# Two attention layers on one core: how exponent products, scores and projection copies are dealt out near the end and the beginning of the attention phase

## The chip, the cores and the metric

The kernel runs on one core of a Trainium2 chip. The metric is the device time of one execution in microseconds; lower is better. The engines are named as the profile names them: PE (TensorE matmuls; PEld are its weight loads), DVE (VectorE), ACT (ScalarE), POOL (GpSimd) and SP (SyncE, which issues most DMAs).

## The reference, cut to what matters

`x` has 2048 tokens of 576 features. Four residual steps follow each other: attention, a spectral filter, attention, a spectral filter. Everything that the change touches lies in the attention step:

```
h   = layernorm(x)
q,k,v = (h @ wqkv) split in 32 heads of 18
s   = q k^T * 18**-0.5, kept where 0 <= query - key < 256
x   = x + (softmax(s) v) @ wo
```

The spectral step is `x + irfft2(rfft2(layernorm(x)) * W)`.

## The kernel before, in words

`layer_a` is one attention layer and is run twice. Tokens are cut into 16 tiles of 128, heads into 8 groups of four (`NQ`). A work item is numbered x = 16 n + j: group n, tile j; there are NX = 128 of them. A head is addressed by `pair` and `hp`; `hp` chooses rows 0 to 63 or 64 to 127 of the PE array, so that two neighbouring matmuls of different `hp` run side by side.

Each score is computed twice. `score_max(x, pair, hp)` (tile `S`, line 1172) multiplies 128 queries by up to 384 keys, and DVE takes the masked row maximum (line 1174). When the four tiles of a chunk have their maxima, `m_rows(n, c)` turns them with one PE transpose (`tpm`, line 1185), ACT negates them into `mt` (line 1187), and two DMAs (line 1189, from SP) write them as an extra row of the stacked queries `qs`. `exps(x, pair, hp)` (tile `E`, line 1205) multiplies 128 keys by the queries of tiles x, x+1 and x+2; that extra row subtracts the maximum, and ACT takes the exponent (line 1206) into a tile `P`. So exponents of x need the maxima of tile x+2, by way of that transpose, ACT and DMA. In the order listings `E118_0` is the product for x = 118; its second number is 2·hp + pair, and `S124_1_0` is x, pair, hp. `tpm7_2` is the transpose of group 7, chunk 2, that is of tiles 120 to 123.

`part` multiplies `P` with the values into the bank `U` (line 1225); after each fourth tile DVE transposes `U` into `us` (line 1230). `divide`, `back` and `store` scale it, turn it back (`o`) and send it off; for group 7 `store` is four DMAs from SP into `o7` (line 1254). `pack` copies group results inside DRAM (line 1258), and `attended` loads them (`oraw`).

The projections of q and k for later groups are cut into units of 14 matmuls into a bank `pj` (line 1109). After a unit, ACT copies it (line 1121, and for later units a second copy, line 1124), and a remainder is subtracted by DVE or POOL (line 1127) and stored.

PSUM has eight banks: three for `S`, three for `E` (some projection units and transposes use them too), one `pj`, one `U`.

All engines run in the order in which the program records work. `opening` records the scores of the first LEAD = 10 items and 70 projection matmuls. `bursts` then records bursts: one score, three exponent products, two scores (scores run ten items ahead), after which come value products, pieces of projection units and, from burst 139 on, when the projections are all done, value products alone. There are 158 bursts; they cover exponents up to x = 117 (MIX = 118) and all scores. The tail loop (from line 1440 on) records the exponents of x = 118 to 127, four at a time, with the value products two tiles behind. Then `out.early` begins the output projection (`ops`, line 802). `behind(t)` is called as the exponents of t are recorded, and issues the loads and splits for the output projection (lines 744 to 780).

Of the kernel before, what the change touches and what calls it, by code (L numbers as in the profile page):

```python
# [8 lines left out]
F32 = mybir.dt.float32  # L9
F32R = mybir.dt.float32r  # L10
BF = mybir.dt.bfloat16
AF = mybir.ActivationFunctionType
# [3 lines left out]
S, D = 2048, 576  # L16
# [699 lines left out]
class Out:  # L716
# [149 lines left out]
def layer_a(tc, ident, eps, bp, big, src, dst, wqk_d, wv_d, wo_d, dc_d, gc_d, dram, copy, wvs, second, spectral, share):  # L866

    nc = tc.nc
    V, A, T, P = nc.vector, nc.scalar, nc.tensor, nc.gpsimd
# [14 lines left out]
    if True:  # L884
# [191 lines left out]
        with ExitStack() as c2:  # L1076
            wp = c2.enter_context(tc.tile_pool(name="a2", bufs=2))
            pp = Banks(tc, c2, "a2p", ("S", "pj"))
# [10 lines left out]
            ended = []  # L1089

            def remainders():
                while ended:
                    ended.pop(0)()

            def proj(i, c, bank=0):

                box = {}
                ks = k_steps()
                cs = slice(c * 512, c * 512 + 512)

                def mm(s, k):
                    wk, p, xk = k
                    if s == 7 and c == 2 and 0 < i < 8:
                        w_split(i + 1)
                    if s == 0:
# [3 lines left out]
                    T.matmul(box["ps"].rearrange("r (n p) -> r n p", n=NT) if second else box["ps"], w[:, wk], x, start=s == 0, stop=s == len(ks) - 1)  # L1109
                    if s == len(ks) - 1:  # L1110
                        if 4 * i + c < 12:

                            sg = wp.tile([128, 4, 384], F32, tag="P", name=f"sg{i}_{c}", bufs=6)
                            sg = sg.rearrange("r a b -> r (a b)")[:, 0:1024].rearrange("r (a t) -> r a t", a=2).bitcast(F32R)
                        else:
                            sg = wp.tile([128, 2, 512], F32R, tag="sg", name=f"sg{i}_{c}", bufs=2)
                        by, rest = box["ps"], sg
                        if second:
                            by = by.rearrange("r (n p) -> r p n", n=NT)
                            rest = sg.rearrange("r a (p n) -> r a p n", n=NT)  # L1120
                        A.copy(rest[:, 0], by)  # L1121
                        aside = 4 * i + c >= 14
                        if aside:
                            A.copy(rest[:, 1].bitcast(F32), by)

                        def remainder():
                            (P if aside else V).tensor_sub(sg[:, 1] if aside else rest[:, 1], sg[:, 1].bitcast(F32) if aside else by,  # L1127
                                                           (sg if aside else rest)[:, 0].bitcast(F32))

                            (nc.scalar if i < 2 else nc.sync).dma_start(qk_d[:, 128 * i:128 * i + 128, cs].rearrange("a r t -> r a t").bitcast(F32), sg.bitcast(F32))  # L1130
                        ended.append(remainder)
                return [lambda s=s, k=k: mm(s, k) for s, k in enumerate(ks)]

            vts = {}
# [55 lines left out]

            pt = {}

            def exps(x, pair, hp):
# [9 lines left out]
                ps = pp.tile([128, 512], F32, name=f"E{x}_{hl_}", **(dict(tag="S", bufs=3) if pair and NX - LEAD <= x else dict(tag="E", bufs=3)))  # L1203
                b = 64 * hp
                T.matmul(ps[:, 0:nq], k[b:b + 64, pair, j * 128:j * 128 + 128], q[b:b + 64, pair, j * 128:j * 128 + nq], start=True, stop=True)  # L1205
                A.activation(p[:, hl_, 0:nq], ps[:, 0:nq], AF.Exp, scale=SC)  # L1206
# [7 lines left out]
            us = {}  # L1214

            def part(x, half):
                n, i = divmod(x, NT)
# [107 lines left out]
            def source(p):  # L1325
                x, half = p
                i = x % NT
                return x - 1 if half == 0 else x - 2 + 2 * (i % 2)

            def bursts():  # L1330

                es = [(x, pair, hp) for x in range(MIX) for pair in range(2) for hp in range(2)]
                ss = [(x + LEAD, pair, 1 - hp) for x, pair, hp in es]
                parts = [(x, half) for x in range(MIX - 2) for half in range(2) if x % NT]
                values = {(4 * x + 7) // 3 + 2 for x in range(0, MIX - 2, 2)}
                ends = [3] + [max(k - 1 for k in values if k - 1 <= 4 + 134 * (i + 1) // 22) for i in range(22)]
                unit = {k: i for i, end in enumerate(ends) for k in range(ends[i - 1] + 1 if i else 0, end + 1)}
                at = 70
                for k in range(-(-len(es) // 3)):
                    e, c = es[3 * k:3 * k + 3], ss[3 * k:3 * k + 3]  # L1340
# [9 lines left out]
                    remainders()  # L1350

                    new, took = [], 0
                    spread = at == len(pj)
                    while parts and (took < 430 or source(parts[0]) < e[0][0] - 3 if spread else took == 0 or parts[0][0] % 2 or parts[0][1]):
                        if (4 * source(parts[0] if spread else (parts[0][0] | 1, 1)) + 3) // 3 + 2 > k:
# [10 lines left out]
                    tasks = [] if took and not spread or 3 * k + 3 >= len(es) else due[:1]  # L1366
                    del due[:len(tasks)]
                    n = 0
                    if k in unit and k not in values:
# [10 lines left out]
                        yield f  # L1380
                    at += n

                    full = (3 * k + len(e)) // 4 + LEAD - 1
# [18 lines left out]
            def behind(t):  # L1402
# [14 lines left out]
                if t - OB + 8 in range(0, 10, 2):  # L1417
                    out.load_x(((t - OB + 8) // 2 + 1) % 5)
# [16 lines left out]
            V.memset(U, 0.0)  # L1435
            for f in bursts():
                f()
                done += 1
            now = -(-4 * MIX // 3)
# [86 lines left out]
```

## Time and profile before

| what | value |
|---|---|
| median of 3 runs | 1331.53 us (1329.79 to 1331.54) |
| the profiled execution's own time | 1330.75 us |
| its span, first to last instruction | 1328.8 us |
| first layer: bursts from, value products end | 127.9, 456.6 us |
| second layer: bursts from, value products end | 806.4, 1136.4 us |
| PE busy | 1294.7 us (97%) |

A busy PE is not a PE at its peak, since the ends of matmuls are modelled: a wait shorter than the length of a matmul does not show as idle time. It shows as a later start, so starts are compared rather than gaps.

### The profile page before, as it was taken

Reading aid. Unit: us, or ns where it says so; the run is one execution under the profiler, and the core shown is the slowest. Engines: PE = TensorE matmul, PEld = TensorE weight load, DVE = VectorE, ACT = ScalarE, POOL = GpSimd, SP = SyncE. Lnnn points to the kernel's source line nnn. Section 1 sums busy time; section 2 is a strip of 40 time slices with the busy share of each in tenths; the row PEclk is TensorE's granted clock in tenths of the full one; section 3 lists DMA queues with packets and bytes.
Section 4 is the critical chain, followed back from the end, with each engine's and each line's share of the span. In section 5 each row is a group of like instructions: output and inputs, shape, how many; then the busy total and the mean of one; then the engine's idle time right before and its main releaser. Section 6 shows DMA issues by size and latency. Waiting matters only on the chain.

```text
span 1328.8 us, 33094 instructions
## 1 busy us (share of the span) xinstructions
PE 1294.7 (97%) x10911; PEld 956.4 (72%) x10911; DVE 948.4 (71%) x3136; ACT 753.1 (57%) x1896; POOL 714.1 (54%) x1200
## 2 busy tenths in 40 slices
PE   9999999999999999999999999999999999899998
PEld 8986666666665599975999975666666654798587
DVE  5417888888889587766674158888888887575855
ACT  5622776777767645543355325677766778574233
POOL 3258566776667443467221295567667667213821
PEclk9999999999999899999999999999999999999999
DMA  6857665765557737688873468566556658497874
GB/s 205 215 156 204 221 199 188 235 195 185 189 163 240 220 116 228 197 274 254 282 246 76 103 207 220 189 213 185 181 176 195 188 173 280 141 336 267 297 253 163
DMA packets 179487, 274.22 MB, mean 206 GB/s; under 512 B 67743, under 2 KB 77727, under 8 KB 177989
## 3 DMA queue, kind: packets, MB, share of 16 engines
q1 hardware_dynamic: 167007, 243.63, 58.5%
q0 software_dynamic: 4656, 13.44, 4.0%
q10 hardware_dynamic: 7654, 15.03, 3.3%
q8 instruction: 88, 1.44, 0.5%
q14 instruction: 82, 0.67, 0.2%
HBM read 164.54 MB, written 114.81 MB: 210 GB/s over the span
## 4 chain that ended last, share of the span: by engine, by line
PE 86%; DVE 5%; issue 3%; DMA 3%; ACT 2%; SPq 1%; POOL 0%; DVEq 0%; ACTq 0%; POOLq 0%
PE pj L1109 20%; PE S L1172 13%; PE U L1225 12%; PE vps L1005 9%; PE ops L802 6%; PE E L1205 6%; PE po L274 4%; PE pq L524 3%; PE p L503 2%; PE pf L274 2%; PE pi L600 2%; PE pz L312 1%; DVE jk L1174 1%; PE tpm L1185 1%; DVE us L1230 1%
## 5 line engine op out<-in xcount | busy, mean ns | idle before, releaser
L1174 DVE CUSTOM_DVE_ANT_0 jk<-S,mask 128x384 bf16<-128x384 f32 (+2 forms) x1024 | 488.5, 526 | 72.4 <-PE S L1172 38.0
L1206 ACT ACTIVATE P<-E 128x384 f32<-128x384 f32 (+2 forms) x1024 | 407.7, 479 | 171.0 <-PE E L1205 130.1
L1172 PE MATMUL S<-ks,qs 63*128 63x384 f32 (+2 forms) x1024 | 280.7, 374 | 3.5 <-DVE m L1174 1.3
L1208 POOL TENSOR_SCALAR_AFFINE_SELECT P<-P 128x512 f32<-128x512 f32 x256 | 163.3, 638 | 195.4 <-ACT P L1206 183.6
L1172 PEld LDWEIGHTS S<-ks,qs 63*128 63x128 f32 x1024 | 146.2, 184 | 117.8 <-DVE m L1174 89.3
L1205 PE MATMUL E<-qs,ks 64*128 64x384 f32 (+2 forms) x1024 | 222.2, 375 | 2.0 <-ACT P L1206 1.9
L1225 PE MATMUL U<-P,vq 128*19 128x128 f32 (+1 forms) x3840 | 190.7, 331 | 4.6 <-DVE us L1230 4.5
L1225 PEld LDWEIGHTS U<-P,vq 128*19 128x19 f32 x3840 | 96.6, 99 | 83.5 <-issue 20.3
L1109 PE MATMUL pj<-xh,wqh 128*128 128x512 f32 x360 | 155.4, 432 | 0.6 <-DVE sg L1127 0.4
L1211 POOL TENSOR_SCALAR_AFFINE_SELECT P<-P 128x512 f32<-128x512 f32 x224 | 143.2, 639 | 0.0
L1205 PEld LDWEIGHTS E<-qs,ks 64*128 64x128 f32 x1024 | 115.1, 186 | 16.3 <-ACT P L1206 10.0
L1109 PE MATMUL pj<-xh,wql 128*128 128x512 f32 x360 | 122.1, 415 | 0.0
L1109 PE MATMUL pj<-xl,wqh 128*128 128x512 f32 x288 | 119.6, 415 | 0.0
L802 PE MATMUL ops<-oroom 128*128 128x290 f32 (+1 forms) x812 | 114.0, 297 | 2.3 <-DVE ofree L848 1.2
L802 PEld LDWEIGHTS ops<-oroom 128*128 128x128 f32 x812 | 110.4, 189 | 2.9 <-ACT ofree L836 2.5
L1109 PEld LDWEIGHTS pj<-xh,wqh 128*128 128x128 f32 x360 | 67.6, 188 | 31.6 <-issue 13.8
L1174 DVE DVE_READ_ACCUMULATOR2_ANT m<- 128x1 f32 x1024 | 85.3, 83 | 0.0
L1121 ACT CAST sg<-pj 128x512 fp32r<-128x512 f32 x72 | 42.4, 589 | 73.2 <-PE pj L1109 65.1
L1109 PEld LDWEIGHTS pj<-xh,wql 128*128 128x128 f32 x360 | 64.2, 188 | 21.9 <-issue 10.8
L1230 DVE STREAM_TRANSPOSE us<-U 128x512 f32<-128x512 f32 x64 | 45.9, 716 | 30.6 <-PE U L1225 30.5
L1109 PEld LDWEIGHTS pj<-xl,wqh 128*128 128x128 f32 x288 | 54.2, 188 | 16.8 <-issue 9.0
L789 POOL TENSOR_TENSOR oroom<-oraw,oroom 64x128 fp32r<-64x128 f32 x26 | 14.0, 537 | 94.9 <-ACT oroom L787 44.4
(510 smaller groups left out, 2278.4 us busy)
## 6 DMA issues: line engine op xcount, KB each, us to landing
qk_d<-sg SPq DMA_DIRECT2D x56, 512.0 KB
qs<-qk_d SPq DMA_DIRECT2D x384, 72.0 KB
ks<-qk_d SPq DMA_DIRECT2D x348, 72.0 KB
op_d<-o SPq DMA_DIRECT2D x56, 256.0 KB
v_d<-vt SPq DMA_DIRECT2D x32, 304.0 KB
vq<-v_d SPq DMA_DIRECT2D x16, 608.0 KB
wt<-in_w SPq DMA_DIRECT2D x16, 580.0 KB
ofree<-x SPq DMA_DIRECT2D x16, 580.0 KB
```

The costliest lines, as they stand in the source:

```text
L274: T.matmul(ps[:, c, 0:NF], tail[r] if si == 4 else hl_(si), dcs[b // 2][r, b % 2], start=mi == si == 0, stop=si == 4)
L802: self.nc.tensor.matmul(self.ps[u][n][:, 0:self.n], x, self.w[p][:, (2 * wk + n) * self.n:(2 * wk + n + 1) * self.n], start=first and i == ...
L1005: T.matmul(ps[:, n, 0:288], xT(xk, c), w[:, wk, n * 288:(n + 1) * 288], start=i == 0, stop=i == len(ks) - 1)
L1109: T.matmul(box["ps"].rearrange("r (n p) -> r n p", n=NT) if second else box["ps"], w[:, wk], x, start=s == 0, stop=s == len(ks) - 1)
L1172: T.matmul(ps[:, 0:N], q[b:b + 63, pair, i * 128:i * 128 + 128], k[b:b + 63, pair, lo:hi], start=True, stop=True)
L1174: V.tensor_tensor_reduce(out=jk[:, 0:N], in0=ps[:, 0:N], in1=mask[:, 384 - N:384], scale=1.0, scalar=-3e38, op0=ALU.add, op1=ALU.max, accu ...
L1205: T.matmul(ps[:, 0:nq], k[b:b + 64, pair, j * 128:j * 128 + 128], q[b:b + 64, pair, j * 128:j * 128 + nq], start=True, stop=True)
L1206: A.activation(p[:, hl_, 0:nq], ps[:, 0:nq], AF.Exp, scale=SC)
L1208: P.affine_select(out=p[:, :, 0:128], in_=p[:, :, 0:128], pattern=[[0, 4], [1, 128]], compare_op=ALU.is_ge, fill=0.0, base=0, channel_mult ...
L1211: P.affine_select(out=p[:, :, 256:384], in_=p[:, :, 256:384], pattern=[[0, 4], [-1, 128]], compare_op=ALU.is_gt, fill=0.0, base=0, channel ...
L1225: T.matmul(U[32 * h:32 * h + 19, (q0 % 4) * 128:(q0 % 4) * 128 + 128 * (q1 - q0)], vts[n][:, j, h], pt[n, j][:, h, (q0 - j) * 128:(q1 - j) ...
L1230: V.transpose(u, U.rearrange("r (p n) -> r n p", n=NT))
```

## The change

1. `MIX` goes from 118 to 121. Twelve bursts hold four exponent products to three scores; the tail has seven items instead of ten. The fourth product of such a burst is put into the `pj` bank.
2. In bursts where the first score and the first exponent would use the same half of the array, the first two scores change places.
3. For projection units that need two copies, the copies are recorded after the next burst's exponents rather than when the unit ends.
4. The third product of the first burst uses bank `U`. `U` is zeroed by ACT in the second burst, no longer by DVE ahead of the first. In the first burst the remainder of the last unit is recorded after the first score.
5. The last two weight splits (`split`, k = 3 and 4) move from x = 116 and 118 to 122 and 124 and wholly to DVE; the x loads are redistributed accordingly.

```diff
-        self.nc.scalar.copy(self.w["h"][:, c], self.raw[:, c])
+        (self.nc.vector.tensor_copy if k > 2 else self.nc.scalar.copy)(self.w["h"][:, c], self.raw[:, c])
...
-                        A.copy(rest[:, 0], by)
                         aside = 4 * i + c >= 14
-                        if aside:
-                            A.copy(rest[:, 1].bitcast(F32), by)
+
+                        def copies():
+                            A.copy(rest[:, 0], by)
+                            if aside:
+                                A.copy(rest[:, 1].bitcast(F32), by)
...
+                        if aside:
+                            ended.append((copies, remainder))
+                        else:
+                            copies()
+                            ended.append((lambda: None, remainder))
...
+                if pair and x >= MIX:
+                    tag = "S"
...
+            def sums():
+                nonlocal U
+                U = pp.tile([128, 512], F32, tag="U", name="U", bufs=1)
+                A.activation(U, eps.to_broadcast([128, 512]), AF.Copy, scale=0.0)
...
-            MIX = 118
+            MIX = 121
...
+                extra, width = len(es) - len(ss), -(-len(ss) // 3)
+                first4 = width - extra - 5
...
+                    plan.append((es[ne:ne + (4 if first4 <= k < first4 + extra else 3)], ss[3 * k:3 * k + 3]))
...
+                    if c[0][2] == e[0][2]:
+                        c = c[1::-1] + c[2:]
                     score_max(*c[0])
-                    for f in e:
-                        exps(*f)
+                    if k == 0:
+                        remainders()
+                    for z, f in enumerate(e):
+                        exps(*f, "U" if k == 0 and z == 2 else "pj" if z == 3 else "E")
+                    for copies, _ in ended:
+                        copies()
...
-                    while parts and (took < 430 or source(parts[0]) < e[0][0] - 3 if spread else took == 0 or parts[0][0] % 2 or parts[0][1]):
+                    while parts and (took < (430 if len(e) < 4 else 640) or source(parts[0]) < e[0][0] - 3 if spread else took == 0 or parts[0][0] % 2 or parts[0][1]):
...
-                if 0 <= t - (OB - 10) < 10 and t % 2 == 0:
-                    out.split((t - (OB - 10)) // 2)
+                if t - OB in (-10, -8, -6, 2, 4):
+                    out.split((-10, -8, -6, 2, 4).index(t - OB))
...
-            U = pp.tile([128, 512], F32, tag="U", name="U", bufs=1)
-            V.memset(U, 0.0)
```

Four-product bursts are 141 to 152, out of 0 to 157.

On PE, where the maxima of tiles 120 to 123 are turned and the exponents of x = 118 first read them, the order before has these rows (a name behind "waits" is a counter; DMAHW ones are those of DMAs from SP):

```order
L1205 MATMUL E114_1_7259<-qs1_1059,ks1_1061 128x384 [waits DMAHW3_49,Activation_49]
L1185 MATMUL tpm7_2_7274<-ident_76,m7_2_7055 16x128
L1172 MATMUL S124_1_0_7283<-ks1_1061,qs1_1059 128x384 [waits DVE_49]
L1205 MATMUL E114_3_7287<-qs1_1059,ks1_1061 128x384 [waits Activation_49]
L1205 MATMUL E115_0_7293<-qs1_1059,ks1_1061 128x384 [waits Activation_49]
...
L1205 MATMUL E117_3_7416<-qs1_1059,ks1_1061 128x384 [waits Activation_49]
L1205 MATMUL E118_0_7427<-qs1_1059,ks1_1061 128x384 [waits DMAHW4_49,Activation_49]
L1205 MATMUL E118_2_7430<-qs1_1059,ks1_1061 128x384 [waits Activation_49]
```

The same place of the changed program, on PE:

```order
L1240 MATMUL U_1619<-P7_2_7200,vq7_6575 19x256 [waits Pool_49]
L1240 MATMUL U_1619<-P7_2_7200,vq7_6575 19x256 x3
L1193 MATMUL tpm7_2_7345<-ident_76,m7_2_7083 16x128 [waits Activation_49]
L1180 MATMUL S124_1_0_7355<-ks1_1061,qs1_1059 128x384 [waits DVE_49]
L1215 MATMUL E117_3_7359<-qs1_1059,ks1_1061 128x384
L1215 MATMUL E118_0_7365<-qs1_1059,ks1_1061 128x384 [waits DMAHW0_49]
L1215 MATMUL E118_2_7368<-qs1_1059,ks1_1061 128x384
L1180 MATMUL S125_0_0_7371<-ks1_1061,qs1_1059 128x384 [waits DVE_49]
```

Between the transpose `tpm7_2` and `E118_0`, which waits for the DMA that this transpose feeds, there stood thirteen exponent products and thirteen scores; now there are one score and one product. `E114_0` and `tpm7_1` came closer in the same way, and so did these on PE and SP. PE, the last chunk of maxima, in the changed program:

```order
L1180 MATMUL S127_1_0_7486<-ks1_1061,qs1_1059 128x384 [waits DVE_49]
L1215 MATMUL E120_3_7490<-qs1_1059,ks1_1061 128x384 [waits Activation_49]
L1215 MATMUL E121_0_7500<-qs1_1059,ks1_1061 128x384 [waits Activation_49]
...
L1215 MATMUL E121_3_7521<-qs1_1059,ks1_1061 128x384 [waits DVE_49]
L1193 MATMUL tpm7_3_7529<-ident_76,m7_3_7309 16x128 [waits DVE_49]
L1215 MATMUL E122_0_7538<-qs1_1059,ks1_1061 128x384 [waits DMAHW5_49,Activation_49]
```

SP, the DMAs that carry those maxima and what stands ahead of them or behind, before:

```order
L774 DMA oraw1_7245<-o_d_85 128x4x256
L1189 DMA qs1_1059<-mt7_3_7451 2x4x128 x2
L766 DMA ofree_6831<-in_x 128x576
L1258 DMA o_d_85<-op_d_86 16x2304 x2
L1254 DMA ofree_6831<-o7_0_7465 18x512 x4
```

SP at the same place, changed:

```order
L774 DMA oraw1_7231<-o_d_85 128x4x256
L1269 DMA ofree_6831<-o7_0_7484 18x512 x4
L1273 DMA o_d_85<-op_d_86 16x2304 x2
L1197 DMA qs1_1059<-mt7_3_7531 2x4x128 x2
L777 DMA oraw0_7189<-o_d_85 64x4x256 x2
```

The four stores of `o7_0` and two copies `o_d` stood behind the maxima's DMAs and now stand ahead of them; the first store waits for DVE's transpose `o7_0`, which DVE does just ahead of the last maximum.

More of the change, by code (lines that the diff above doesn't have):

```diff
@@ L1092, in remainders @@
                 while ended:
-                    ended.pop(0)()
+                    copies, remainder = ended.pop(0)
+                    copies()
+                    remainder()
             def proj(i, c, bank=0):
@@ L1191, in layer_a, with exps @@
             pt = {}
-            def exps(x, pair, hp):
+            def exps(x, pair, hp, tag="E"):
                 n, j = divmod(x, NT)
@@ L1201, in exps @@
                 p = pt[n, j]
-                ps = pp.tile([128, 512], F32, name=f"E{x}_{hl_}", **(dict(tag="S", bufs=3) if pair and NX - LEAD <= x else dict(tag="E", bufs=3)))
+                if pair and x >= MIX:
+                    tag = "S"
+                ps = pp.tile([128, 512], F32, tag=tag, name=f"E{x}_{hl_}", bufs=3 if tag in "ES" else 1)
                 b = 64 * hp
@@ L1330, in bursts @@
             def bursts():
[L1332 to L1333 removed]
+                es, ss = [[(x, pair, hp) for x in r for pair in range(2) for hp in order] for r, order in ((range(MIX), (0, 1)), (range(LEAD, NX), (1, 0)))]
+                extra, width = len(es) - len(ss), -(-len(ss) // 3)
+                first4 = width - extra - 5
+                plan, ns = [], 0
+                for k in range(width):
+                    ne = sum(len(e) for e, _ in plan)
+                    plan.append((es[ne:ne + (4 if first4 <= k < first4 + extra else 3)], ss[3 * k:3 * k + 3]))
+                made = {x: k for k, (e, _) in enumerate(plan) for x, *_ in e}
+                assert sum(len(e) for e, _ in plan) == len(es)
                 parts = [(x, half) for x in range(MIX - 2) for half in range(2) if x % NT]
[L1335 removed]
+                values = {made[x + 1] + 2 for x in range(0, MIX - 2, 2)}
                 ends = [3] + [max(k - 1 for k in values if k - 1 <= 4 + 134 * (i + 1) // 22) for i in range(22)]
+                assert ends[-1] < first4
                 unit = {k: i for i, end in enumerate(ends) for k in range(ends[i - 1] + 1 if i else 0, end + 1)}
                 at = 70
[L1339 to L1340 removed]
+                for k, (e, c) in enumerate(plan):
+                    if k == 1:
+                        sums()
                     for x, pair, hp in e:
@@ L1364, in bursts @@
                             later(k, *divmod(x // 4, 4))
-                    tasks = [] if took and not spread or 3 * k + 3 >= len(es) else due[:1]
+                    tasks = [] if took and not spread or k == len(plan) - 1 else due[:1]
                     del due[:len(tasks)]
@@ L1381, in bursts @@
                     at += n
-                    full = (3 * k + len(e)) // 4 + LEAD - 1
+                    full = (3 * k + len(c)) // 4 + LEAD - 1
                     if (3 * k) // 4 + LEAD - 1 < full and full % 4 == 3:
@@ L1416, in behind @@
                     out.filters()
-                if t - OB + 8 in range(0, 10, 2):
-                    out.load_x(((t - OB + 8) // 2 + 1) % 5)
+                if t - OB in (-8, -6, -4, 2, 4):
+                    out.load_x(((-8, -6, -4, 2, 4).index(t - OB) + 1) % 5)
                 if 0 <= t - (OB - 8) < 6:
@@ L1438, in layer_a @@
                 done += 1
-            now = -(-4 * MIX // 3)
+            now = -(-4 * (NX - LEAD) // 3)
             later.lags = 1, 3, 4
```

10 lines of the change are left out of this document (6 added, 4 removed).

## The prediction

> **What bounds the kernel now.** I read the page first, then a table of stretches over the end of each attention phase, then the single rows there. The page says that PE is the bound over the whole:
>
> ```profile
> PE 1294.7 (97%) x10911; PEld 956.4 (72%) x10911; DVE 948.4 (71%) x3136; ACT 753.1 (57%) x1896; POOL 714.1 (54%) x1200
> ```
>
> That is an average. I cut the end of each phase at five times: the start of burst 141, the start of burst 153, the end of the last row maximum, the start of the product E122_0, and the first output projection. Columns are microseconds and instructions by engine, then PE's granted clock, the DMA engines' share and GB/s; first layer, then second:
>
> ```profile
> core 0: us, PE busy (x) PEld busy (x) DVE busy (x) ACT busy (x) POOL busy (x), PEclk, DMA share, GB/s
> 407.27:428.18 20.91, 20.13 (x224) 11.19 (x221) 20.84 (x80) 15.31 (x41) 15.48 (x24) 1.00 0.74 230
> 428.18:437.64 9.46, 7.30 (x75) 3.87 (x77) 9.31 (x35) 7.55 (x19) 6.42 (x11) 1.00 0.99 341
> 437.64:445.71 8.07, 8.07 (x79) 3.59 (x73) 2.70 (x7) 5.35 (x14) 3.29 (x6) 0.58 0.89 314
> 445.71:456.64 10.93, 10.31 (x155) 5.32 (x153) 6.21 (x12) 10.52 (x28) 8.84 (x14) 1.00 0.86 202
> ...
> 1087.66:1108.55 20.89, 19.99 (x223) 11.01 (x220) 20.81 (x80) 15.41 (x41) 15.45 (x24) 1.00 0.76 244
> 1108.55:1117.44 8.89, 7.32 (x73) 3.87 (x76) 8.75 (x35) 7.46 (x18) 6.98 (x11) 0.99 0.98 331
> 1117.44:1124.37 6.93, 6.93 (x80) 3.42 (x72) 2.72 (x7) 5.03 (x14) 3.10 (x6) 0.77 1.04 359
> 1124.37:1136.36 11.99, 10.44 (x155) 5.53 (x153) 3.88 (x9) 10.93 (x30) 8.43 (x14) 1.00 0.61 165
> ```
>
> Up to the last maximum DVE has no idle time (20.81 of 20.89 us, 8.75 of 8.89), and in the second stretch the DMA engines are full (0.98). After it DVE is nearly idle and the clock dips; in the last stretch ACT is full in the second layer but for 1.1 us. So in the bursts that get a fourth product, DVE is the bound and not PE.
>
> **The beginning of the bursts: a gain.** These rows are from the first layer's bursts 0 and 1:
>
> ```profile
> 128.00 0.59 ACT L1121 CAST sg<-pj 128x512 fp32r<-128x512 f32 x1 [3.04 <-PE pj L1109]
> 128.18 0.48 DVE L1435 MEMSET U<- 128x512 f32 x1 [0.18 <-DVE m L1174]
> 129.03 0.18 PEld L1205 LDWEIGHTS E<-qs,ks 64*128 64x128 f32 x1 [0.84 <-ACT P L1206]
> 130.50 0.69 DVE L1127 TENSOR_TENSOR sg<-pj,sg 128x512 fp32r<-128x512 f32 x1
> 131.75 0.18 PEld L1205 LDWEIGHTS E<-qs,ks 64*128 64x128 f32 x1 [0.76 <-ACT P L1206]
> ```
>
> One `E` bank is still held by the projection that the subtraction at 130.50 reads, so the third product of either burst stands for 0.84 and 0.76 us. With bank `U` for one and the subtraction before the other, both go: 1.6 us. The subtraction (0.69) now delays two maxima, the removed memset (0.48) brings them forward. I take **1.5 us a layer**, 1.1 to 1.6. Zeroing by ACT (never seen here; bounded by zero and the 0.59 of a cast of that size) lies behind the three exponents of burst 0, and burst 1's own wait for their products covers it.
>
> **The copies behind the exponents: a small gain.** Where a short burst follows the end of a unit:
>
> ```profile
> 219.81 1.26 ACT L1206 ACTIVATE P<-E 128x384 f32<-128x384 f32 x3 [0.36 <-PE E L1205]
> 221.48 0.59 ACT L1121 CAST sg<-pj 128x512 fp32r<-128x512 f32 x1 [0.20 <-PE pj L1109]
> 221.96 0.59 ACT L1124 COPY sg<-pj 128x512 f32<-128x512 f32 x1
> 222.44 2.43 ACT L1206 ACTIVATE P<-E 128x384 f32<-128x384 f32 x6
> ...
> 222.88 0.44 PE L1172 MATMUL S<-ks,qs 63*128 63x384 f32 x1
> 223.00 1.20 PE L1205 MATMUL E<-qs,ks 64*128 64x384 f32 x3
> 223.77 0.61 PE L1172 MATMUL S<-ks,qs 63*128 63x384 f32 x2
> 224.31 0.50 PE L1109 MATMUL pj<-xh,wqh 128*128 128x512 f32 x1
> ...
> 225.64 0.44 PE L1172 MATMUL S<-ks,qs 63*128 63x384 f32 x1
> ...
> 226.37 0.41 PE L1225 MATMUL U<-P,vq 128*19 128x256 f32 x4
> ```
>
> The burst from 222.88 lasts 1.43 us to its projection at 224.31. The next one, unhindered, lasts 0.73 (225.64 to 226.37), so the copies cost 0.7. Moved, three exponents run first, from 221.83 at 0.38 apart; the copies start at 222.98 and 0.48 later and end at 224.05. The next unit's first matmul, due at 223.61, needs the copied bank and now waits for that: 0.2 is left of the 0.7. This happens three times a layer, and once more just before burst 139, where no unit follows (0.5 of 0.7, the rest lost to DVE). Together **1.1 us a layer**, 0 to 2.8.
>
> **The end: the lead of scores over exponents shrinks from ten items to seven.** DVE does the same maxima, and before the last one loses a split (0.72 between starts) and gains one transpose (0.70), one reciprocal (0.25) and one product (0.48): **+0.6**. The split copies that leave ACT run on DVE in the tail, where it is idle: nothing, and up to 0.7 each without that cover. The cost lies in the rows of maxima, whose way to `qs` is this in the second layer:
>
> ```profile
> 1108.34 0.28 PE L1185 MATMUL tpm<-ident,m 128*16 128x128 f32 x1
> 1108.66 0.27 ACT L1187 ACTIVATE mt<-tpm 16x128 fp32r<-16x128 f32 x1 [0.49 <-PE tpm L1185]
> 1108.95 1.13 SPq L1189 DMA_DIRECT2D qs<-mt  x2
> ```
>
> From transpose to issue 0.61 us. No row gives the landing of SP's DMAs; POOL's small ones bound it:
>
> ```profile
> o_d<-op_d POOLq DMA_DIRECT2D x48, 144.0 KB, 3.8
> ks<-qk_d POOLq DMA_DIRECT2D x36, 72.0 KB, 4.8
> ofree<-ye POOLq DMA_DIRECT2D x7, 18.1 KB, 2.6
> ```
>
> 2.6 to 4.8; with the DMA engines 0.98 full I take 3.8. Now E118_0 follows its transpose after one score and one product (0.3 us). PE stands about 4 us, and behind E118_0 stand S125 and all later scores, for which DVE waits. DVE idles 0.61 + 3.8, plus 0.65 until the next score reaches it, less the 0.3 and less the 1.2 of maxima still waiting: **3.6**. E114 has one burst (1.74 us, 20.89 over 12) between transpose and use, against 4.4: a stall of 2.4, of which 1.2 to 1.7 is covered in the same way; **0.7**. The last maximum thus ends 0.6 + 3.6 + 0.7 = 4.9 later.
>
> From there to E122_0 stands SP's queue:
>
> ```profile
> 1120.37 1.12 SPq L1189 DMA_DIRECT2D qs<-mt  x2
> 1121.98 1.19 SPq L1258 DMA_DIRECT2D o_d<-op_d  x2
> 1123.94 3.45 SPq L1254 DMA_DIRECT2D ofree<-o  x4
> ```
>
> The four stores and two copies (3.45 + 1.19) are now ahead of the maxima's DMAs and start some 0.5 before the last maximum ends: its DMA issues 4.1 us after, lands in 2.6 (now little is queued), and E122_0 starts at 6.7. Before, it started 6.93 after in the second layer and 8.07 in the first (the third stretches of the table): **−0.2 and −1.4**. From E122_0 on all work is as before, 10.9; the second layer loses its wait for `oroom`, **−1.1**:
>
> ```profile
> 1136.36 0.40 PE L802 MATMUL ops_pj<-oroom 128*128 128x290 f32 x1 [1.12 <-DVE oroom L787]
> ```
>
> Last, the clock. Before, it falls to half after short waits at the tail's start and is back ahead of E122_0: 0.58 over 8.07 us is 6.8 us at half speed, 0.77 over 6.93 is 3.2. Now PE stands some 6 us right ahead of E122_0, and a dip of that kind falls on the stretch that was at full clock. An item of the tail at half and at full clock:
>
> ```profile
> 441.25 1.01 PE L1205 MATMUL E<-qs,ks 64*128 64x384 f32 x4
> ...
> 443.60 0.69 PE L1205 MATMUL E<-qs,ks 64*128 64x384 f32 x2
> ...
> 448.55 0.90 PE L1205 MATMUL E<-qs,ks 64*128 64x384 f32 x4
> ...
> 450.15 0.82 PE L1205 MATMUL E<-qs,ks 64*128 64x384 f32 x4
> ```
>
> 2.35 against 1.60: 0.75 each, for about two items: **+1.5** a layer, 0 to 2.3. A dip after E118 I cost at nothing, since DVE is the bound there; without that cover the 5.3 us of PE work up to the last score would double for as long as the dip lasts, some 1.5.
>
> **The sum.** The end costs 4.9 − 1.4 + 1.5 = +5.0 in the first layer and 4.9 − 0.2 − 1.1 + 1.5 = +5.1 in the second. Beginning and copies give back 2 × (1.5 + 1.1) = 5.2. Net +4.9 us: from the profiled execution's own 1330.75 (span 1328.8) to **1335.6 us**. That execution lies 0.8 below the median of the runs, 1331.53; against it the forecast is +0.3%. About 0.2%, 2.7 us, is what a measurement of this kernel can tell from no change.
>
> **The rivals.** *The rows of maxima come in time: faster.* Place: E114, E118 and E122; mechanism: the 4 KB DMAs of SP are not held up by what is queued ahead. With a landing of 1.6 instead of 3.8 the last maximum ends 2.2 earlier for E118 and 0.7 for E114, and E122 follows 1.0 sooner: 3.9 a layer, 1327.8. It decides from a landing of 1.9 downward. For it: the rows are tiny. Against it: the smallest transfer whose landing the profile gives, 18.1 KB, took 2.6, and the DMA engines are full. Chance 0.20.
>
> *Waits and gains cancel: no change.* With 2.6 at E118 and E114 the last maximum ends 1.9 earlier (1.2 and 0.7), and the total falls by 3.8 to 1331.8. For it: the 2.6 of the small transfer; and E118's own data were not yet needed in the rows before, so its lateness is worked out, not seen. Chance 0.25. The Trainium skill's page "DMA: Bandwidth & Descriptors" (section "Anatomy of one DMA — SWDGE (gpsimd) path") gives some 2.0 us as fixed cost of a transfer, which no row here reaches. By it alone, an estimate, the sum would be 1329.4.
>
> *The queue is fuller than before: slower still.* Loads that `behind` spread over 1.33 bursts an item now come at one item a burst, and the DMA share before was 0.98 already. With 4.8 at all three places the last maximum ends 1.5 later and E122_0 2.2 after that, and a dip after E118 costs 1.5: 5.2 a layer, 1346. Chance 0.13.
>
> *ACT becomes the bound in the four-product bursts.* Four exponents at 0.38, their latency 0.12 and a quarter of an `mt` (0.27) make 1.7 against DVE's 1.74; the fourth shares the bank of the transposes, so that each may wait. At 0.3 a burst this is 12 × 0.3 × 2 = 7 us, 1343. Chance 0.05.
>
> **How the numbers follow.** The forecast has 0.37. It and the two slower cases give 0.55 for slower by over 0.2%; no change 0.25, faster 0.20. The ends of all unknown costs taken together reach from 1325 (no dip, all of the copies' 0.7, 2.6 everywhere) to beyond 1346. Leaving out one in ten on either side I give 1327 to 1343; the forecast's own range is 1333 to 1339. What decides is one number, the time from a maximum's transpose to the product that reads its row; everything else is under 2 us a layer.
>
> **What the changed profile would show.** Bursts 0 and 1 without the waits of 0.84 and 0.76. A first projection matmul after a short burst that waits some 0.5 for ACT's second copy. PE idle for about 4 us at E118_0 and 6 us at E122_0, released by `qs<-mt`; DVE idle with it, where it was full; the four stores of `o` ahead of the last `qs<-mt` on SP, and a half clock in the last stretch. I am wrong if DVE stays full up to the last maximum and PE's waits at E118 and E122 are under 2 us: then the end costs little or gains. I am wrong in the other direction if POOL's or ACT's part of the four-product bursts makes them longer than 2 us.

## The result, and the profile after

The changed kernel takes 1344.44 us (median of 4 runs, 1343.61 to 1346.92) against 1331.24 us before (median of 4, 1329.79 to 1331.54): a ratio of 1.0104, with a 95% interval of 1.0087 to 1.0122. It is slower by 13 us, where the forecast was slower by 5 and its range ended at 1343. The profiled execution took 1346.92 us (span 1344.8), 16.2 more than the profiled one of before. It is the longest of its four, so the 16 us that the stages below add up to are 3 more than the difference of the medians; all readings below are of this pair.

The group table of the page shows where to look. First the products `E` of the page before, then of the page after; the last columns are busy time, mean ns of one, and the idle time of PE ahead of them with what ended most of it:

```profile
L1205 PE MATMUL E<-qs,ks 64*128 64x384 f32 (+2 forms) x1024 | 222.2, 375 | 2.0 <-ACT P L1206 1.9
```

```profile
L1215 PE MATMUL E<-qs,ks 64*128 64x384 f32 (+2 forms) x1024 | 221.0, 376 | 25.1 <-DMA qs<-mt 23.2
```

PE's idle time ahead of the exponent products grew from 2.0 us, 1.9 of it put down to ACT, to 25.1, and 23.2 of that is the wait for the rows of maxima. The stretches of the changed trace at the same five places (burst 141, burst 153, end of the last maximum, E122_0, first output projection), first layer, then second, with the columns of the table in the prediction:

```profile
408.13:434.14 26.01, 23.93 (x267) 13.40 (x263) 22.28 (x85) 20.92 (x55) 19.94 (x31) 0.93 0.83 266
434.14:448.84 14.70, 9.60 (x97) 5.21 (x100) 8.86 (x31) 5.98 (x15) 4.75 (x8) 0.77 0.69 237
448.84:455.06 6.22, 0.89 (x15) 0.34 (x8) 4.70 (x10) 1.69 (x5) 2.53 (x4) 0.76 0.26 72
455.06:467.12 12.06, 11.67 (x152) 5.67 (x152) 4.65 (x9) 9.69 (x25) 6.70 (x10) 0.84 0.84 212
...
1097.20:1122.68 25.48, 22.80 (x267) 12.72 (x263) 22.16 (x85) 20.99 (x55) 19.92 (x31) 1.00 0.86 280
1122.68:1135.63 12.95, 9.32 (x97) 5.05 (x100) 8.78 (x31) 5.97 (x15) 4.76 (x8) 0.74 0.72 243
1135.63:1141.88 6.25, 0.90 (x16) 0.34 (x9) 4.71 (x10) 1.69 (x5) 2.52 (x4) 0.70 0.27 72
1141.88:1154.90 13.02, 12.65 (x152) 5.83 (x153) 4.70 (x9) 9.83 (x25) 6.68 (x10) 0.75 0.77 197
```

DVE, which was full up to the last maximum, now idles: 3.7 of 26.01 us and 5.8 of 14.70 in the first layer. From the last maximum to E122_0 PE is idle but for 0.9 us. And the half clock, before only behind the last maximum, now falls on all four stretches of the first layer and on three of the second. Stage by stage (lengths of the stretches; the forecast's 2.6 for the first is the beginning and the copies together):

| us | layer 1: before, after | layer 2: before, after | change | forecast |
|---|---|---|---|---|
| burst 0 to burst 141 | 279.37, 280.61 | 281.22, 278.88 | +1.2, −2.3 | −2.6, −2.6 |
| burst 141 to the last maximum | 30.37, 40.71 | 29.78, 38.43 | +10.3, +8.7 | +4.9, +4.9 |
| last maximum to E122_0 | 8.07, 6.22 | 6.93, 6.25 | −1.9, −0.7 | −1.4, −0.2 |
| E122_0 to the output projection | 10.93, 12.06 | 11.99, 13.02 | +1.1, +1.0 | +1.5, +0.4 |
| all between and behind | | | −1.5 | 0 |

The sum is 16.0, the difference of the spans; the forecast's is 4.9. The rows of PE that hold the stalls, first layer E112_0, E118_0 and E122_0, second layer E114_0, E118_0 and E122_0 (a product's name is found by its place in the order):

```profile
420.97 0.68 PE L1215 MATMUL E<-qs,ks 64*128 64x384 f32 x3 [1.04 <-DMA qs<-mt]
...
433.94 0.28 PE L1193 MATMUL tpm<-ident,m 128*16 128x128 f32 x1
434.14 0.44 PE L1180 MATMUL S<-ks,qs 63*128 63x384 f32 x1
434.15 0.44 PE L1215 MATMUL E<-qs,ks 64*128 64x384 f32 x1
439.65 0.69 PE L1215 MATMUL E<-qs,ks 64*128 64x384 f32 x2 [5.07 <-DMA qs<-mt]
...
455.06 0.69 PE L1215 MATMUL E<-qs,ks 64*128 64x384 f32 x2 [5.33 <-DMA qs<-mt]
...
1115.17 0.59 PE L1215 MATMUL E<-qs,ks 64*128 64x384 f32 x3 [1.69 <-DMA qs<-mt]
...
1122.48 0.28 PE L1193 MATMUL tpm<-ident,m 128*16 128x128 f32 x1
...
1126.72 0.69 PE L1215 MATMUL E<-qs,ks 64*128 64x384 f32 x2 [3.59 <-DMA qs<-mt]
...
1141.88 0.69 PE L1215 MATMUL E<-qs,ks 64*128 64x384 f32 x2 [5.35 <-DMA qs<-mt]
```

From tpm7_2 to E118_0 go 5.71 and 4.24 us, with one score and one product between, as the order listing had it. SP's queue in the first layer shows the other two places:

```profile
413.99 3.96 SPq L1155 DMA_DIRECT2D ks<-qk_d  x6
418.05 1.10 SPq L1197 DMA_DIRECT2D qs<-mt  x2
...
434.55 1.14 SPq L1197 DMA_DIRECT2D qs<-mt  x2
...
448.43 3.18 SPq L1269 DMA_DIRECT2D ofree<-o  x4
451.71 1.18 SPq L1273 DMA_DIRECT2D o_d<-op_d  x2
452.99 1.23 SPq L1197 DMA_DIRECT2D qs<-mt  x2
```

The rows of tpm7_0, which PE turned at 411.94, stand behind the loads of the last group's keys until 418.05 (E112_0 waits for them); those of tpm7_3 stand behind the four stores and two copies until 452.99; those of tpm7_2 stand behind nothing on SP and still take 5.1 us from issue to E118_0.

### The profile page after: what moved, and what is told of

Its sections match the earlier page's. It is cut to its first block, busy times and chain, and to the rows that moved or that the text cites. A ratio compares the mean times of both kernels' runs of the same rounds, so it can differ in the third digit from the quotient of the medians.

```text
span 1344.8 us, 33105 instructions
## 1 busy us (share of the span) xinstructions
PE 1291.9 (96%) x10911; PEld 954.1 (71%) x10911; DVE 949.9 (71%) x3138; ACT 751.6 (56%) x1894; POOL 712.2 (53%) x1200
## 4 chain that ended last, share of the span: by engine, by line
PE 83%; DMA 5%; DVE 4%; ACT 3%; issue 2%; POOL 1%; SPq 1%; DVEq 0%; ACTq 0%; POOLq 0%
PE pj L1111 19%; PE S L1180 13%; PE U L1240 12%; PE vps L1005 8%; PE ops L802 6%; PE E L1215 5%; PE po L274 4%; PE pq L524 2%; PE p L503 2%; DMA qs<-mt 2%; PE pf L274 2%; PE pi L600 2%; ACT P L1216 1%; PE pz L312 1%; DMA qk_d<-sg 1%
## 5 line engine op out<-in xcount | busy, mean ns | idle before, releaser
L1215 PE MATMUL E<-qs,ks 64*128 64x384 f32 (+2 forms) x1024 | 221.0, 376 | 25.1 <-DMA qs<-mt 23.2
L1131 POOL TENSOR_TENSOR sg<-sg 128x512 fp32r<-128x512 f32 x44 | 56.5, 1285 | 30.0 <-ACT sg L1128 29.5
```

## The experiments

Ratios are of each kernel's runs to runs of the kernel before on the same chip, with a 95% interval. Two of the profiled executions (`end_only` and `rows_act`) were the shortest of their kernel's runs, some 5 us below its median, so their times say more than their traces' lengths.

### Which part costs: the end alone, the beginning and copies alone

`end_only` undoes the beginning and the copies in the changed kernel. Its edit at the copies:

```
-                        if aside:
-                            ended.append((copies, remainder))
-                        else:
-                            copies()
-                            ended.append((lambda: None, remainder))
+                        copies()
+                        ended.append((lambda: None, remainder))
```

At the beginning `sums()` and its call go, the memset of `U` returns ahead of the bursts, and all third products use bank `E`.

> The changed kernel with its beginning and its copies put back as before; what is left of the change is the end: the four-product bursts, the shorter lead and the moved loads and splits. Theory (the end alone makes the loss, by waits for the rows of maxima): 12 to 17 us slower than before, 1343 to 1348 us, with the same stalls of PE, 3.5 to 5 us ahead of E118_0 and some 5 us ahead of E122_0 in either layer. Rival (the beginning and the copies, which gained nothing in the trace, make a good part of the loss): under 8 us slower, below 1339.

Measured: 1.0124 (1.0093 to 1.0156), 1347.03 us; the first layer stalls 1.7, 2.75 and 5.5 us at E114_0, E118_0 and E122_0, the second 2.3, 3.0 and 5.2. At E118_0 that is less than the 3.5 to 5 expected, and at E114_0 there is a stall that was not. The end alone makes the whole loss.

`start_and_copies` keeps the other half:

```
-            MIX = 121
+            MIX = 118
```

and the old items for splits and loads.

> The changed kernel with MIX back at 118 (no burst has a fourth product) and loads and splits back at their old items; what is left is the beginning and the copies. Theory: no more than 0 to 3 us faster than before (1328 to 1331), since in the changed trace the waits of bursts 0 and 1 are gone (1.6 us a layer) but a DMA that had slack takes most of it back by E5_0. Rival (the copies behind the exponents cost, as the late pj copies near E104 hint): 1332 to 1336.

Measured: 0.9989 (0.9971 to 1.0008), 1328.54 us. The 5.2 us of the forecast lie outside (the interval is −3.9 to +1.1 us). The two parts alone, each in the kernel before:

> The kernel before with the beginning alone: the third product of burst 0 in bank U, the sums zeroed by ACT behind it, the subtraction ahead of the maxima. Theory (the prediction's mechanism holds, 1.6 us a layer at E0_1 and E1_2, and up to 1.2 us of it are lost again at E4_3 and E5_0, whose exponents wait for the store of a projection block whose buffer they take): 1 to 3 us faster than before. Rival (all of it is lost again, as in the first layer of the changed kernel): within 1 us.

> The kernel before with the copies of a unit behind the next exponents, and nothing else of the change. Theory (the wait only moves: 0.35 us earlier at the third product of a short burst, 0.43 later at the next unit's first matmul, three times a layer, and 0.5 lost by E104_3): 1 to 2 us slower than before. Rival (the prediction: 1.1 us a layer gained): 2 us faster.

Measured: `a_only` 0.9998 (0.9986 to 1.0010), `b_only` 1.0004 (0.9993 to 1.0015). In us the intervals are −1.9 to +1.3 and −0.9 to +2.0. Neither part gains what the forecast gave it (3.0 and 2.2); whether the copies cost one microsecond stays open. The trace of `a_only` shows one place where the beginning's gain is lost. ACT in the second layer, by start, duration and idle time ahead:

```profile
816.17 0.49 ACT L1213 ACTIVATE P<-E 128x384 f32<-128x384 f32 x1 [0.16 <-PE E L1212]
819.33 2.13 ACT L1213 ACTIVATE P<-E 128x384 f32<-128x384 f32 x5 [2.67 <-DMA qk_d<-sg]
```

Bursts 0 and 1 lose their waits: E1_2 starts 1.61 us earlier than before. Four items on, the exponents of a new tile `P` take a buffer that still holds a projection block `sg` on its way to DRAM, and ACT waits for that store; PE then waits 1.17 for ACT at E4_3, and the clock falls to half behind it (0.66 over the stretch from 820 to 830). What ends last there is not PE's work but a transfer that had little slack. The loss is not the same everywhere: measured from burst 0, the products behind burst 1 start 1.4 us earlier than before; by E6_0 1.0 of it is lost again in the first layer of `a_only`, in its second layer all of it and 3.2 more, and nothing in the second layer of `start_and_copies`. The changed kernel has the same wait of ACT, 1.8 us, in both layers (at 140.92 and 830.24).

### Is it the waits, or the four-product bursts themselves?

`rows_aside` writes the last group's rows of maxima to a spare tile, so its exponents read rows of an earlier group; every instruction and DMA is still there.

```
+                if n == NQ - 1:
+                    spare = wp.tile([16, 128], F32, tag="spare", name=f"spare{c}", bufs=2)
+                    for pair in range(2):
+                        nc.sync.dma_start(spare[8 * pair:8 * pair + 8], mt[8 * pair:8 * pair + 8].bitcast(F32))
+                    return
```

> The changed kernel, but the rows of maxima of the last group are written to a spare tile, so that no exponent product of that group waits for them (its exponents then use the rows of an earlier group). All instructions and DMAs are still there. Theory (these waits are the whole cost of the end): E112_0 to E122_0 stall for under 1 us each and the time falls below that of the kernel before, 1314 to 1324 us. Rival (the four-product bursts themselves are slower, by ACT, POOL or a fuller DMA queue): above 1330.

Measured: 0.9957 (0.9941 to 0.9972), 1323.62 us, 6 below the kernel before and, by the two ratios, some 20 below the changed kernel. Its stretches at the same places, first layer, then second:

```profile
405.91:429.30 23.39, 22.64 (x268) 12.84 (x265) 21.98 (x85) 20.67 (x55) 19.75 (x31) 1.00 0.82 268
429.30:437.95 8.65, 8.19 (x97) 4.48 (x100) 8.62 (x31) 5.75 (x15) 4.80 (x9) 1.00 1.06 365
437.95:438.78 0.83, 0.83 (x16) 0.32 (x8) 0.46 (x3) 0.80 (x3) 0.78 (x2) 1.00 1.03 375
438.78:449.46 10.68, 10.43 (x153) 5.32 (x153) 7.00 (x13) 10.19 (x28) 9.26 (x13) 1.00 0.72 218
...
1080.40:1103.87 23.47, 22.64 (x267) 12.81 (x263) 21.96 (x85) 20.71 (x55) 19.73 (x31) 1.00 0.79 252
1103.87:1112.53 8.66, 8.21 (x97) 4.48 (x100) 8.62 (x31) 5.75 (x15) 4.83 (x9) 1.00 1.07 375
1112.53:1113.36 0.83, 0.83 (x17) 0.32 (x9) 0.47 (x3) 0.79 (x3) 0.78 (x2) 1.00 1.09 373
1113.36:1124.70 11.34, 10.48 (x153) 5.28 (x152) 6.79 (x13) 10.60 (x29) 9.35 (x13) 1.00 0.73 228
```

This prices each wait. Against it the changed kernel is longer by 2.6 and 2.0 us in the first stretch (E112_0 and E114_0), by 6.05 and 4.3 in the second (E118_0), and by 5.4 in the third of either layer (E122_0). The clock stays full in all of it: the half clock is a consequence of the waits too. No product of that group stalls for these rows any more. Without them the bursts themselves bring the last maximum 1.7 and 2.35 us later than before, and the whole end is 5.8 and 4.4 us shorter.

### The queue, or the load on the DMA engines?

`rows_act` lets ACT issue the last group's rows, past SP's queue; `last_act` does that for the last chunk alone:

```
-                    (nc.sync if n or c > 1 else nc.scalar).dma_start(q[63::64 ...
+                    (nc.sync if 0 < n < NQ - 1 or n == 0 and c > 1 else nc.scalar).dma_start(q[63::64 ...
```

```
-                    (nc.sync if n or c > 1 else nc.scalar).dma_start(q[63::64 ...
+                    (nc.scalar if n == 0 and c < 2 or n == NQ - 1 and c == 3 else nc.sync).dma_start(q[63::64 ...
```

> The changed kernel, but the DMAs of the last group's rows of maxima are issued by ACT, which made them, instead of SP, so that they stand behind nothing in SP's queue. Theory (a good part of the wait is the queue: 3 us of SP's stores ahead at E122_0, earlier loads ahead at E112_0, E114_0 and E118_0): the stall ahead of E122_0 falls from 5.3 to 2.5 us, that ahead of E118_0 from 5.1 and 3.6 to under 3; 1333 to 1339 us. Rival (the time is the latency of a small DMA, whatever its queue): E118_0 stalls as before, only E122_0 gains; 1338 to 1342.

> The changed kernel, but only the last chunk's rows of maxima (the ones E122_0 waits for) are issued by ACT; SP keeps the others. Theory (SP's four stores and two copies stand ahead of them): the stall ahead of E122_0 falls from 5.3 to 2.7 us in either layer, nothing else moves, 1337 to 1341 us. Rival (the time comes back at once, since E122_0 is not what the end waits for): the stall falls but the first output projection comes no earlier; 1343 to 1347.

Measured: `rows_act` 1.0126 (1.0098 to 1.0155), `last_act` 1.0082 (1.0056 to 1.0108). E122_0's stall fell to 2.7 in both kernels and both layers, as the queue theory has it. PE in the first layer of `last_act`:

```profile
452.19 0.44 PE L1215 MATMUL E<-qs,ks 64*128 64x384 f32 x2 [2.70 <-DMA qs<-mt]
```

The times say less. `last_act` took 1339.6 us, inside its range, but its interval overlaps the changed kernel's (1.0087 to 1.0122), so that its gain in time is not clear of noise; and not all else stood still, since its E112_0 stalled 3.7 us in the first layer and 1.6 in the second. `rows_act` took 1348.4 us, above the ranges of both its theory and its rival, although its E112_0 and E114_0, whose rows had stood behind loads on SP, no longer wait for them. Why it is not faster stays open; its trace shows that ACT, which now issues the rows, takes no exponent for 1.1 us each time. And in `rows_act` E118_0 stalled as before. Its ACT and PE:

```profile
435.77 1.08 ACTq L1197 DMA_DIRECT2D qs<-mt  x2
```

```profile
439.81 0.69 PE L1215 MATMUL E<-qs,ks 64*128 64x384 f32 x2 [4.00 <-DMA qs<-mt]
```

Issued from a queue with nothing ahead, the rows still need 4.0 us to E118_0 (4.6 in the second layer, against 5.1 and 3.6 by way of SP). So at E118_0 SP's queue was not the cause; the DMA engines' share in those 4.0 us was 0.98. A rule of the Trainium skill, page "DMA: Bandwidth & Descriptors", section "Queues, rings and completion order", agrees with this: a transfer's completion is counted only when every earlier write of the same DMA engine has landed, across its queues. No run here tells that rule from a plain lack of free time on the engines.

`loads_early` tests the load itself: the six 0.5 MB loads of `oraw` are issued four items earlier.

```
-                if 0 <= t - (OB - 8) < 6:
-                    out.attended(*divmod(t - (OB - 8), 2))
+                if 0 <= t - (OB - 12) < 6:
+                    out.attended(*divmod(t - (OB - 12), 2))
```

> The changed kernel with six loads of oraw (0.5 MB each, 3 MB) issued four items earlier, so that they are through when tpm7_2's rows are issued. Theory (what holds the 4 KB up is the DMA engines' load, whose share is 1.07 in the stall before E118_0): rows of tpm7_2 land under 3 us after their issue, E118_0 stalls under 3 us instead of 5.1 and 3.6; 1337 to 1342 us. Rival (a fixed time of such a transfer, whatever else runs): E118_0 stalls as before; 1343 to 1346. If the load only moves forward, E112_0 and E114_0 stall more instead.

Measured: 1.0201 (1.0175 to 1.0227), 1356.17 us, slower than all others, yet the place under test behaves as the load theory says. SP, PE, and two stretches of the first layer, one around tpm7_1's rows and one around tpm7_2's:

```profile
425.44 1.14 SPq L1197 DMA_DIRECT2D qs<-mt  x2
...
440.74 1.14 SPq L1197 DMA_DIRECT2D qs<-mt  x2
```

```profile
442.40 0.44 PE L1215 MATMUL E<-qs,ks 64*128 64x384 f32 x2 [1.61 <-DMA qs<-mt]
```

```profile
423.70:430.90 7.20, 3.42 (x32) 1.91 (x28) 2.80 (x9) 2.95 (x7) 3.79 (x5) 0.74 1.03 345
440.10:442.40 2.30, 0.65 (x4) 0.28 (x5) 1.25 (x5) 0.76 (x2) 1.51 (x3) 1.00 0.12 46
```

With the DMA engines quiet (share 0.12) the same rows need 1.66 us from issue to E118_0 (1.65 in the second layer), instead of 5.1 and 3.6. The loads had not gone, though; they now lay on tpm7_1's rows (share 1.03, 345 GB/s), and E114_0 stalled 3.8 us where it had stalled 0.4. E112_0 stalled 2.5, and E122_0 5.5 as before. The time rose, as the last sentence of the expectation allowed.

### How much lead is needed

`mix119` and `mix120` change one number:

```
-            MIX = 121
+            MIX = 119
```

> The changed kernel with MIX = 119: four bursts with a fourth product instead of twelve, so the lead of scores over exponents shrinks by one item only. Theory (a stall is the 5 to 6 us from a transpose to the landing of its rows, less the work that PE has between): about three bursts, 5 us, stand between tpm7_2 and E118_0, so E118_0 stalls under 1 us, and E122_0, with half as much work ahead of it as before, 1 to 3 us; 1328 to 1334 us. Rival (each four-product burst costs by itself, a third of the loss for a third of the bursts): 1334 to 1337, with no matching stall.

> The changed kernel with MIX = 120: eight bursts with a fourth product, the lead shrinks by two items. Theory: some 2.5 us of work stand between tpm7_2 and E118_0, so E118_0 stalls 2 to 3 us and E122_0 3 to 4.5; 1335 to 1341 us. Rival (cost by burst, two thirds of the loss): 1339 to 1342, in proportion.

Measured: `mix119` 0.9980 (0.9967 to 0.9992), 1326.34 us; `mix120` 1.0063 (1.0042 to 1.0085), 1337.63. The cost is not in proportion to the bursts: a third of them costs nothing, two thirds over half. In `mix119` E118_0 does not stall, and E122_0 stalls 2.8 and 2.45; in `mix120` E118_0 stalls 3.1 and 2.9. (E122_0 there stalled 1.9 and 2.6, less than the 3 to 4.5 that were expected, and E112_0 2.4 in the second layer, which was not expected.) Of the kernels that compute all of the reference, `mix119` is the first whose interval lies below the kernel before, by 0.2%. With its copies put back:

> mix119 with the copies put back to where they were. Theory: 1 to 2 us less than mix119, so 3 to 5 us less than before. Rival: the copies do gain, and it is 1 to 2 us slower than mix119.

Measured: 0.9976 (0.9959 to 0.9993), 1326.73 us, not to be told from `mix119`. The last stall of `mix119`, at E122_0, falls in a stretch with a DMA share of 0.92:

```profile
435.78:441.78 6.00, 3.21 (x43) 1.57 (x41) 3.42 (x8) 4.29 (x12) 4.40 (x8) 1.00 0.92 314
```

So `mix119_late` moves 1.25 MB of loads behind the last rows:

```
-                if t == OB - 3:
+                if t == OB + 3:
                     out.filters()
...
-                if 0 <= t - (OB - 8) < 6:
+                if 0 <= t - (OB - 8) < 4:
                     out.attended(*divmod(t - (OB - 8), 2))
                 if t - OB in (1, 2):
+                    out.attended(2, t - OB - 1)
                     out.attended(3, t - OB - 1)
```

> mix119 with three bulk loads (the last two of oraw, 0.5 MB each, and the filters, 0.25 MB) issued behind the last rows of maxima instead of ahead of them. Theory (the load of the DMA engines sets the landing): tpm7_3's rows land under 3 us after the transpose's copy is issued instead of 4, E122_0 stalls under 1.5 us instead of 2.8 and 2.45, and the time is 3 to 7 us below mix119. Rival (the loads are then late for the output projection): E122_0 comes earlier, but the time is not below mix119.

Measured: 1.0031 (1.0019 to 1.0043), 1333.77 us. E122_0 no longer stalls in either layer: its rows go out at 437.52 and it starts 1.83 later, where `mix119` needed 4.78 (437.00 to 441.78). The load was its cause too; it was not SP's queue, which issued nothing between 434.87 and 437.00 in `mix119`. The rival was right about the time. PE in the first layer, at the first output projection:

```profile
454.47 0.40 PE L802 MATMUL ops_pj<-oroom 128*128 128x288 f32 x1 [3.73 <-DVE oroom L787]
```

The projection now waits 3.7 us (1.2 in the second layer) for DVE, which turns what those loads bring, and later products of it wait 0.5 and 2.7 for ACT. Neither place that was tried was free: moved forward, loads hold up tpm7_1's rows; moved back, they hold up the projection. A smaller move, or loads in smaller pieces around the rows, was not tried.

## Why the prediction came out as it did, point by point

- **The direction and its mechanism were right.** The lead fell from ten items to seven, the order put E118_0 one score and one product behind its transpose, and PE and DVE stood there and ahead of E122_0. `rows_aside` shows that these waits are all of the loss and more.
- **The step that failed most: "The last maximum thus ends 0.6 + 3.6 + 0.7 = 4.9 later".** It ended 10.3 and 8.7 later. Term by term, by `rows_aside`: the work of the bursts 1.7 and 2.35 for the 0.6; E118_0 6.05 and 4.3 for the 3.6; E114_0 with E112_0 2.6 and 2.0 for the 0.7. *The work:* in `rows_aside` DVE is busy only 0.45 and 1.0 longer than before up to the last maximum, but it idles 1.4 and 1.5 us in the four-product bursts, which the prediction took for full. *E118_0:* from transpose to product went 5.71 us in the first layer, more than the 5.4 that its rows allowed at most (0.61 + 4.8), and 4.24 in the second, for the 4.4 taken. The larger part was the cover, "less the 1.2 of maxima still waiting". DVE had about 0.5:

```profile
440.70 0.56 DVE L1182 CUSTOM_DVE_ANT_0 jk<-S,mask 128x384 bf16<-128x384 f32 x1 [5.51 <-PE S L1180]
...
1127.77 0.56 DVE L1182 CUSTOM_DVE_ANT_0 jk<-S,mask 128x384 bf16<-128x384 f32 x1 [4.04 <-PE S L1180]
```

Without any cover the prediction's own sum gives 5.71 + 0.65 − 0.3 = 6.06 and 4.24 + 0.65 − 0.3 = 4.59. That the stalls at E112_0 and E114_0 had used the rest up is likely, since DVE had waited 3.3 and 2.9 us for scores and products ahead of there; no run separates it.
- **E112_0 was missing.** The chain was followed from the second chunk of the last group on; the first chunk's rows stand behind the loads of that group's keys on SP (418.05 after a transpose at 411.94). Before, they went out at 417.30 and E112_0 came at 421.21, late enough for them.
- **E122_0 was right, term by term.** Its rows went out 4.15 us after the last maximum in the first layer (4.1 forecast) and were used 2.07 later (2.6 taken); 6.2 against 6.7. SP's stores and copies make half of that stall, 5.3 down to 2.7 in `last_act`. From E122_0 on the first layer grew by 1.1 for the 1.5 taken. In the second the wait of 1.1 for `oroom` went as said, and the stretch still grew by 1.0, which leaves 2.1 for the half clock. Against `rows_aside`, whose clock is full there, the stretch is 1.4 and 1.7 longer.
- **"Beginning and copies give back 2 × (1.5 + 1.1) = 5.2" failed.** The waits of 0.84 and 0.76 went as said. Behind them stood a transfer that the sum did not ask for: the store of `sg`, in a buffer that a new `P` needs; what it takes back differs from trace to trace. In the changed trace, the first layer also met two more waits, 0.96 at E2_0 for rows of maxima and 0.86 at E50_0, which the trace puts down to ACT; the second did not and was 2.3 shorter up to burst 141, near the 2.6 forecast. The copies gained 0.1 at a short burst (2.76 us from its start to the next before, 2.63 after: 223.41 to 226.04), half of the 0.2 taken; just before E104 they gained 0.6 where 0.5 was taken, but the next burst lost 0.85 again, for which the sum has no term. In `b_only`'s trace burst 141 still comes 1.0 and 1.45 earlier, with the 1.1 taken in between, but `end_only`, which has none of this, differs by +0.3 and −0.7 there; and `b_only` then waits 2.3 for `oroom` in the first layer and 1.8 for rows of maxima in the second. A gain ahead of the end was met by transfers at the end.
- **The rivals.** Landing in 1.6 us does occur, but where the DMA engines are quiet, which they are not at E118_0. The fuller queue is what happened in kind at E118_0: loads that `behind` issues held up the rows. That its price, 1346 in all, is close to the time is luck: it put 2.2 a layer on E122_0, which came 0.5 earlier than forecast, and 1.5 on the last maximum, which came 5.4 and 3.8 later. ACT did not become the bound: in `rows_aside` it is busy 20.67 of 23.39 us in the four-product bursts, which last 1.95 us each.

Of the 11.1 us between forecast and measured span, 9.2 are the last maximum and 4.1 the beginning and copies; the rest is −2.2.

## What to carry to other kernels

A lead that hides a transfer is spent before it looks spent: price each product that comes nearer to its transfer, the first of a group too, and do not count slack in the engine behind twice when two stalls follow each other. Here the same small transfer took between 1.7 and 5.1 us to its use, by what the DMA engines carried at that moment; look at their share in the stretch where it is due. At E118_0 another queue did not help, and moving the loads cost more elsewhere than it gained, since no quiet stretch was at hand to move them to. Where a wait goes, look for the buffer that is due next and whether a DMA still reads it.

## What the runs showed of the hardware

- The same pair of 4 KB transfers took 1.66 us from issue to use at a DMA share of 0.12 (`loads_early`), 1.83 at 0.23 (`last_act`, E122_0) and 2.07 at 0.50 (the changed trace, E122_0). At E118_0 in the changed trace it took 5.1 in the first layer, while the share was 1.07 and more, and 3.6 in the second. Issued by ACT at a share of 0.98 it took 4.0.

```profile
434.50:437.00 2.50, 0.09 (x2) 0.00 (x0) 0.68 (x3) 0.51 (x2) 1.95 (x4) 1.00 1.07 368
437.00:439.70 2.70, 0.05 (x2) 0.05 (x2) 0.00 (x0) 0.00 (x0) 0.00 (x0) 0.76 1.09 362
```

- The half clock can follow a short wait. Around the 1.04 us stall at E112_0 in the changed trace:

```profile
416.00:419.49 3.49, 3.21 (x46) 1.83 (x42) 3.49 (x13) 2.81 (x10) 2.66 (x5) 1.00 0.68 218
419.49:421.35 1.86, 0.82 (x10) 0.60 (x7) 1.08 (x7) 0.28 (x1) 1.05 (x2) 1.00 0.61 166
421.35:424.76 3.41, 3.41 (x29) 1.83 (x25) 1.46 (x5) 1.90 (x5) 1.57 (x2) 0.50 1.00 332
```

PE had been busy for 4.0 of the 5.35 us ahead, and the granted clock was 0.50 for the next 3.41. The Trainium skill's page "TensorE: Matmul & The Clock Gate", section "What's actually happening", has the clock fall after an idle window of about 3.4 us; here far less idle time was enough, so the measurement decides.
